# Three moves in VectorE's instruction order: a joining of products, two sums of inputs, and two finishing steps

## The chip, the cores and the metric

The kernel runs on one core of a Trainium2 chip. The time is the device time of one execution in microseconds (us); shorter is better. The median of three runs stands for the kernel.

## The reference

Eight samples of 3008 tokens by 256 channels, all in fp32. Each goes through a filter in the frequency domain along the tokens and then through a mixer of two small networks, one along the tokens and one along the channels.

```python
X = np.fft.rfft(x, axis=1)                      # 8 x 1505 x 256
Y = X * (filt_r + 1j * filt_i)[None]
x = np.fft.irfft(Y, n=3008, axis=1)             # the filter
xt = x.transpose(0, 2, 1)
h = np.maximum(xt @ w_tok1, 0.0) @ w_tok2       # 3008 -> 256 -> 3008, along the tokens
u = x + h.transpose(0, 2, 1)
h2 = np.maximum(u @ w_ch1, 0.0) @ w_ch2         # 256 -> 1536 -> 256, along the channels
out = u + h2
```

## The kernel before

**The filter.** 3008 is 47 times 64, and the Fourier transform is done as matmuls over the factor 64 and then over the factor 47. The samples form the groups (0), (1, 2), (3, 4), (5, 6), (7) (`GROUPS`). The generator `dft(bs)` holds the filter's work for one group and is stopped at every `yield`; the letter that it yields names the step that comes next. Sample 0's filter runs at the start; each later group's runs beside the mixer of the group before it. For the last three groups the steps are these.
- `s`: `x_sums` adds and subtracts the two halves of a loaded pair of input blocks on VectorE (two instructions into the tile `sd`, line 548). The input blocks (`x_pair`, into the tiles `filt`) are loaded ahead: three pairs when the group begins.
- `d`, `c`: `a_pair` is the matmuls by the length-64 table (line 523); the results leave through ScalarE and a transfer.
- `b`: `b_pair` is the matmuls by the length-47 table; `products` multiplies by the filter (line 705).
- `m`: `join` subtracts and adds the products of a pair of frequencies (two VectorE instructions on tile `p`, lines 710 and 711), for the inverse length-47 matmuls `bi_pair` (`i`, or ahead of the next `products`).

**The mixer.** `mix` walks over items (sample `b`, tile `m` of up to 512 tokens, pair `jp` of the hidden blocks): 8 x 6 x 6. The number of an item within its sample is `i % n`, with `n` = 36, so the last six items of a sample (30 to 35) are its tail. An item's matmuls stand in this order on TensorE: `up_first` (four, line 984), `down` part 0 of the item before (three, line 1018), `up_last` (three, line 1000), and `down` parts 1 and 2 (two and two, line 1018). All matrix products are fast schemes with seven products in place of eight, so VectorE makes sums around each: `hh` and `s` in `up_middle`, `t` in `h_sums`, `hh` again in `up_last`, all recorded at line 962 (`v`). A matmul of the item waits for the sums ahead of it, and two PSUM banks (`ps_pg`) serve each item in turn. Each fp32 matmul leaves two records in the trace.

When a tile's six items are through, `finish` gives six VectorE steps (`a`, `b_`, `c`, `d`, a transposition, and a second transposition with the stores of the output). They wait in the list `todo_v`; `one_step` takes one from it. In the first sample a step is taken early in an item, ahead of the sums `t`, and a step later in it; in the other samples two are taken later in the item.

**The token product.** In item 32 of each sample but the last, `token_product` runs the next sample's first token matmul as 12 times seven matmuls (line 850). VectorE prepares the sums `ts` for block `j + 2` when block `j` is done. At its end ScalarE copies a part of the result into the tile `c` (line 856), and VectorE makes three sums into `c` out of PSUM; a fourth, the ReLU (ScalarE, line 865) and five sums on GpSimd (`combine`, lines 378 to 382) follow in item 33. Its first readers on TensorE are the matmuls at line 905 in item 34.

**What sets the order.** The program is written out in the order of these Python calls; each engine runs its own instructions in that order. Within an item `mix` yields at the places 0, 1, 1.5 and 2, and the driver at the end of the kernel lets the filter go on one step where the table `due` names the pair (`jp`, place) for the step that comes next. In a tail the step `m` is due at (2, 2), which is after the token product, and the step `s` at (5, 1) alone; in other items `s` is due at (0, 1), (2, 1), (3, 1) and (5, 1). A new group's filter begins at item 32, place 2, of the first, third and fifth sample; there the three pairs of inputs are asked for. In the second, fourth and sixth sample item 32 has a step `m` at that place.

Of the kernel before, what the change touches and what calls it, by code (L numbers as in the profile page):

```python
# [42 lines left out]
JP = JT // 2  # L43
# [3 lines left out]
MT = 6  # L47
# [4 lines left out]
AP = A // 2  # L52
# [75 lines left out]
def kernel(  # L128
# [712 lines left out]
    def token_product(b):  # L841
        one, two = (bank(tag).rearrange("p (s n) -> p s n", n=P) for tag in turn)
        for j in range(AP):
            w, t = w1_ring[:, j % W1S], token_ts[b][:, j % 2]
            r = 2 * j % TC4
            rows = t4[b, 2 * j // TC4][:, r:r + 2].rearrange("p r (e n) -> p (r e) n", e=DH)
            todo = ((one, 0, 0, rows[:, 0]), (one, 1, 1, rows[:, 2]), (two, 2, 5, rows[:, 3]), (one, 3, 6, t[:, 0]),
                    (two, 0, 4, t[:, 1]), (one, 2, 3, t[:, 2]), (two, 1, 2, t[:, 3]))
            for i, (ps, at, n, mov) in enumerate(todo):
                nc.tensor.matmul(ps[:, at], w[:, n], mov, start=(j == 0 and i in (0, 2)), stop=(j == AP - 1 and i >= 5))  # L850
            if j + W1S < AP:
                w1_load(j + W1S)
            if j + 2 < AP:
                t4_sums(b, j + 2)
        c = rp.tile([P, 8, P], FP32, tag="r", name="c")
        nc.scalar.copy(out=c[:, 0], in_=one[:, 0])
        v(c[:, 1:3], one[:, 1:3], c[:, 0:1].to_broadcast([P, 2, P]))
        v(c[:, 3], two[:, 0], c[:, 2])
        v(c[:, 4:8:3], one[:, 3:4].to_broadcast([P, 2, P]), c[:, 2:4])
        h1 = w2[:, 0:1, 7 * 256:].rearrange("p o (s t) -> p o s t", t=P)[:, :, 0:7, :]  # L860

        def finish_h1():
            v(c[:, 5:7], two[:, 1:3], c[:, 3:5])
            for at, to in ((slice(1, 7, 5), slice(0, 5, 4)), (slice(5, 8, 2), slice(1, 7, 5))):
                nc.scalar.activation(out=h1[:, 0, to, :], in_=c[:, at], func=AF.Relu)
            combine(h1)

        todo_h1.append(finish_h1)
        return h1[:, 0]
# [239 lines left out]
    h1s, uts, vts = {}, {}, {}  # L1109
# [22 lines left out]
    def mix(next_ready):  # L1132

        wait = []
        pos, hhs, tts = {}, {}, {}

        def loads(b):
            if b + 1 < B and next_ready(b):
                for c in wait:
                    t4_load(b + 1, c)  # L1140
                wait.clear()


        own = ({(4, 2): (0, 1)}, {(2, 2): (0,), (3, 0): (1,), (3, 2): (2, 3)})
        new = {(JP - 2, 0): (0, 1), (JP - 1, 0): (2, 3)}

        def u_parts(b, m, jp, place):
            parts = own[b > 0] if m + 1 < MT else new if b + 1 < B else {}
            now = parts.get((jp, place), ())
            b, m = (b, m + 1) if m + 1 < MT else (b + 1, 0)  # L1150
            for part in now:
                u_part(b, m, part)
            if now and now[-1] == max(p for ps in parts.values() for p in ps):
                if m:
                    wait.append(m)
                todo_v.extend(v_steps(b, m))
                if b and (b, m) < (B - 1, MT - 2):
                    w2m_load((m + 2) % MT)

        to_dram = [f for m in range(MT) for f in w2_sums(m)]  # L1160
        w1_todo, w1_out = w1_sums()
        items = [(b, m, jp) for b in range(B) for m in range(MT) for jp in range(JP)]
        n = MT * JP
        for i in range(len(items) + 1):
            now, old = i < len(items), i >= 1
            if not now:
                bo, mo, jo = items[i - 1]
                t = tp.tile([P, 4, 256], FP32, tag="t", name="t")
                last_item(bo, mo, jo, hhs.pop(i - 1), t, uts[bo, mo], pos[bo, mo])
                break  # L1170
            if JP - 2 <= i < JP + 2:
                for _ in range(6 if i > JP - 2 else 1):
                    if w1_todo:
                        w1_todo.pop(0)()
            elif i >= 2 * JP and i % 2 and w1_out:
                w1_out.pop(0)()
            if i and ended[0] < len(tiles):
                convert_middle()
                convert_end(False)
                convert_middle()  # L1180
            if now:
                b, m, jp = items[i]
                if i % n == 0:
                    wait.append(0)
                w = width(m)
                hhs[i] = hp.tile([P, 4, 256], FP32, tag="hh", name="hh")
                g = [bank("pg").rearrange("p (s n) -> p s n", s=2) for _ in range(2)]
                s = up_first(jp, uts[b, m], vts[b, m], w, g)
                up_middle(hhs[i], w, g, s)
            while todo_h1:  # L1190
                todo_h1.pop()()
            if i < n:
                one_step()
            if old:
                bo, mo, jo = items[i - 1]
                tts[i - 1] = tp.tile([P, 4, 256], FP32, tag="t", name="t")
                for f in h_sums(hhs[i - 1], tts[i - 1], width(mo)):
                    f()
                down(mo, jo, 0, hhs[i - 1], tts[i - 1], pos.setdefault((bo, mo), []))
            if now:  # L1200
                u_parts(b, m, jp, 0)
            copies()
            yield b, i % n, 0
            if ended[0] < len(tiles):
                if i == 0:
                    convert_middle()
                convert_end(False)
            if now:
                up_last(jp, uts[b, m], vts[b, m], w, g, s, hhs[i])
                if b + 1 < B and i % n == n - 4:  # L1210
                    t4_sums(b + 1, 0)
            one_step()
            if i >= n or i % n == n - 1:
                one_step()
            if now and b + 1 < B:
                if n - 4 - W1S <= i % n < n - 4:
                    w1_load(i % n - (n - 4 - W1S))
                if i % n == n - 4:
                    t4_sums(b + 1, 1)
            copies()  # L1220
            loads(b)
            yield b, i % n, 1
            if old:
                down(mo, jo, 1, hhs[i - 1], tts[i - 1], pos[bo, mo])
            yield b, i % n, 1.5
            if old:
                down(mo, jo, 2, hhs.pop(i - 1), tts.pop(i - 1), pos[bo, mo])
                if jo == JP - 1:
                    todo_v.extend(finish(bo, mo, uts[bo, mo], pos[bo, mo]))
                    one_step()  # L1230
                    one_step()
            if now:
                if b + 1 < B and i % n == n - 4:
                    h1s[b + 1] = token_product(b + 1)
                u_parts(b, m, jp, 2)
                if jp == JP - 1:
                    while todo_v and m + 1 == MT:
                        one_step()
                if i >= 8 and to_dram:
                    to_dram.pop(0)()  # L1240
                if i in (28, 29):
                    w2m_load(i - 28)
            loads(b)
            yield b, i % n, 2
        while todo_v:
            one_step()

    with tc.manual_schedule():
# [61 lines left out]
        group, todo, done = -1, iter(()), True  # L1310
# [6 lines left out]
        coming = "a"  # L1317
        n = MT * JP
        for b, i, place in mix(next_ready):
            at = (b, i, place)  # L1320
            if at == (0, 0, 0) or group + 1 < len(GROUPS) and at == (GROUPS[group][-1], n - 4, 2):
# [3 lines left out]
                done = group + 1 == len(GROUPS)  # L1325
                todo = iter(()) if done else dft(GROUPS[group + 1]) if group else second
                coming = next(todo, "end") if group else "a"
                if group:
                    continue
            if done:  # L1330
                continue
            jp = i % JP
            if coming in "aw":
                due = place == 1 or (place != 1.5 if group == 0 else coming == "w")
            elif group:
                tail = i >= n - JP
                sums_at = ((5, 1),) if tail else ((0, 1), (2, 1), (3, 1), (5, 1))
                due = (jp, place) in {"s": sums_at, "d": ((1, 1.5), (4, 1.5)), "c": ((2, 0), (5, 0)), "b": ((1, 1.5), (3 if tail else 4, 1.5)), "m": ((2, 2) if tail else (3, 1), (5, 1)),
                                      "i": ((0, 1.5), (3 if tail else 4, 1.5))}[coming]
            else:  # L1340
                due = (jp - (coming == "i")) % JP in ((5, 1, 2, 3) if i < 4 * JP else (5, 0, 1, 2, 3)) and place == {"b": 1, "m": 2, "i": 0}[coming]
# [36 lines left out]
```

## Time and profile before

| what | value |
|---|---|
| median of three runs | 2416.26 us (2415.17 to 2418.65) |
| the profiled execution's own time | 2418.01 us |
| its span, first to last instruction | 2416.2 us, clock granted to TensorE 0.996 |
| TensorE (PE) busy | 2374.1 us, 98% |
| VectorE (DVE) busy | 1942.4 us, 80% |
| ScalarE (ACT), GpSimd (POOL) busy | 690.5 us, 29%; 619.2 us, 26% |
| DMA | 278.65 MB, mean 115 GB/s |

A row of a timeline has the start in us from the span's beginning, the length in us, engine, line, operation, output and inputs by their names in the program, shapes, the number of records merged in it, and in brackets the idle time before it with what ended it. A matmul's end in the trace is modelled, so that two busy rows may hide a pause; the distance between starts is measured. A busy share near 100% therefore doesn't show that TensorE never waits.

### The profile page before, as it was taken

How to read it: one execution, taken by the hardware profiler on the slowest of the kernel's cores; microseconds unless marked ns; L12 is line 12 of the kernel's file. 1: busy time of each engine (PE TensorE's matmuls, PEld its weight loads, DVE VectorE, ACT ScalarE, POOL GpSimd, SP SyncE). 2: the span in 40 equal slices, each digit the busy share in tenths (PEclk: the TensorE clock that was granted, in tenths of full speed). 3: DMA queues.
4: the chain of work that ended last, by engine and by line, in shares of the span. 5: the costliest groups of instructions: out<-in, count | busy, mean ns of one | idle time of the engine just before them, and what ended most of it. 6: DMA issues, size and time to landing. Idle time of an engine off the chain costs nothing.

```text
span 2416.2 us, 35472 instructions
## 1 busy us (share of the span) xinstructions
PE 2374.1 (98%) x12340; PEld 1989.5 (82%) x12340; DVE 1942.4 (80%) x3673; ACT 690.5 (29%) x1339; POOL 619.2 (26%) x1115
## 2 busy tenths in 40 slices
PE   7989999999999999999999999999999999999998
PEld 4656676978888888988888888898888988898887
DVE  7798778777887888777788888877888777777776
ACT  5733322232222222123322222213222222222222
POOL 7476332113111211211121112112212112112121
PEclk8999999999999999999999999999999999999999
DMA  9985545534443223534344222344434111311100
GB/s 213 250 234 166 157 142 179 172 122 122 130 134 98 86 78 91 187 97 138 112 132 125 76 81 83 105 161 128 125 106 146 56 60 37 114 63 31 39 15 21
DMA packets 186011, 278.65 MB, mean 115 GB/s; under 512 B 35101, under 2 KB 122859, under 8 KB 185832
## 3 DMA queue, kind: packets, MB, share of 16 engines
q1 hardware_dynamic: 139544, 212.56, 28.7%
q0 software_dynamic: 34688, 53.83, 8.4%
q10 hardware_dynamic: 11600, 10.00, 1.4%
q8 instruction: 98, 1.61, 0.3%
q14 instruction: 81, 0.66, 0.1%
HBM read 193.52 MB, written 82.72 MB: 114 GB/s over the span
## 4 chain that ended last, share of the span: by engine, by line
PE 87%; DVE 6%; DMA 4%; issue 1%; POOL 1%; ACT 1%; SPq 0%; ACTq 0%; DVEq 0%; POOLq 0%
PE ps_po L1018 34%; PE ps_pg L984 19%; PE ps_pg L1000 14%; PE ps_b L523 4%; PE ps_b L850 3%; PE ps_acc L905 3%; PE ps_acc L850 2%; PE ps_b L905 2%; PE ps_pg L523 2%; PE ps_acc L883 2%; PE ps_b L883 2%; DMA st<-in_moe_w_tok_dram 1%; DVE t L962 1%; DVE hh L962 1%; DVE u L962 1%
## 5 line engine op out<-in xcount | busy, mean ns | idle before, releaser
L1026 POOL DMA_DIRECT2D out_dram<-r x752 | 407.9, 550 | 1611.9 <-issue 1149.2
L962 DVE TENSOR_TENSOR hh<-ps_pg,s 128x512 f32<-128x512 f32 (+3 forms) x864 | 482.4, 586 | 193.2 <-ACT s L987 191.3
L1005 ACT ACTIVATE hh<-hh 128x512 f32<-128x512 f32 (+1 forms) x576 | 347.8, 621 | 975.9 <-DVE hh L962 975.9
L1018 PE MATMUL ps_po<-t,wc 128*128 128x256 f32 (+1 forms) x2296 | 551.5, 379 | 1.8 <-DVE t L962 1.8
L1018 PEld LDWEIGHTS ps_po<-t,wc 128*128 128x128 f32 x2296 | 428.3, 190 | 110.2 <-issue 41.8
L984 PE MATMUL ps_pg<-v,wc 128*128 128x256 f32 (+1 forms) x1728 | 413.4, 376 | 1.7 <-POOL wc L381 1.6
L1018 PE MATMUL ps_po<-hh,wc 128*128 128x256 f32 (+1 forms) x1722 | 412.2, 375 | 0.6 <-POOL wc L382 0.6
L984 PEld LDWEIGHTS ps_pg<-v,wc 128*128 128x128 f32 x1728 | 327.9, 190 | 41.7 <-DVE v L962 3.2
L1018 PEld LDWEIGHTS ps_po<-hh,wc 128*128 128x128 f32 x1722 | 327.0, 190 | 39.4 <-POOL wc L382 1.7
L1000 PE MATMUL ps_pg<-u,wc 128*128 128x256 f32 (+1 forms) x1152 | 294.0, 378 | 1.9 <-DVE hh L962 1.3
L962 DVE TENSOR_TENSOR t<-t,hh 128x256 f32<-128x256 f32 (+1 forms) x576 | 246.2, 427 | 19.8
L1000 PEld LDWEIGHTS ps_pg<-u,wc 128*128 128x128 f32 x1152 | 216.3, 190 | 47.9 <-DVE hh L962 18.2
L962 DVE TENSOR_TENSOR s<-ps_pg,hh 128x512 f32<-128x512 f32 (+1 forms) x288 | 196.1, 681 | 30.7 <-DVE hh L962 0.9
L987 ACT COPY s<-ps_pg 128x256 f32<-128x256 f32 (+1 forms) x288 | 105.9, 368 | 343.6 <-PE ps_pg L984 339.3
L962 DVE TENSOR_TENSOR t<-hh 128x512 f32<-128x512 f32 (+1 forms) x288 | 195.4, 678 | 0.6 <-ACT hh L1005 0.6
L984 PE MATMUL ps_pg<-u,wc 128*128 128x256 f32 (+1 forms) x576 | 169.3, 376 | 2.4 <-DVE hh L962 2.4
L1000 PE MATMUL ps_pg<-v,wc 128*128 128x256 f32 (+1 forms) x576 | 168.9, 375 | 0.0
L984 PEld LDWEIGHTS ps_pg<-u,wc 128*128 128x128 f32 x576 | 108.3, 190 | 18.6 <-DVE hh L962 5.5
L1000 PEld LDWEIGHTS ps_pg<-v,wc 128*128 128x128 f32 x576 | 109.1, 190 | 12.7
L962 DVE TENSOR_TENSOR u<-ps_acc,u 128x256 f32<-128x256 f32 (+1 forms) x84 | 46.2, 550 | 80.4 <-PE ps_acc L905 56.9
L962 DVE TENSOR_TENSOR u<-ps_b,u 128x512 f32<-128x512 f32 (+2 forms) x126 | 74.5, 591 | 28.8 <-PE ps_b L905 26.7
L905 PE MATMUL ps_acc<-w 128*128 128x256 f32 (+1 forms) x336 | 85.3, 376 | 0.0
(164 smaller groups left out, 2638.6 us busy)
## 6 DMA issues: line engine op xcount, KB each, us to landing
w<-w_tmp SPq DMA_DIRECT2D x84, 448.0 KB
w<-w_tmp SPq DMA_DIRECT2D x35, 896.0 KB
out_dram<-r POOLq DMA_DIRECT2D x696, 32.0 KB, 2.2
g_tmp<-t SPq DMA_DIRECT2D x112, 192.0 KB
t<-g_tmp SPq DMA_DIRECT2D x42, 512.0 KB
t<-z_tmp SPq DMA_DIRECT2D x180, 96.0 KB
z_tmp<-t SPq DMA_DIRECT2D x60, 256.0 KB
filt<-in_x_dram SPq DMA_DIRECT2D x90, 128.0 KB
```

The lines of the kernel that those rows point to most:

```text
L523: nc.tensor.matmul(outs(i, j), stat(i, j), mov(i, j), start=True, stop=True)
L850: nc.tensor.matmul(ps[:, at], w[:, n], mov, start=(j == 0 and i in (0, 2)), stop=(j == AP - 1 and i >= 5))
L883: nc.tensor.matmul(ps[:, ds(q * P, n)], t4[b, c][:, r, ts(dh, P)], wai[:, 0:n], start=(first and q == 0), stop=(not first and q == 3))
L905: nc.tensor.matmul(ps[:, ds(j * hw, hw)], h1[:, n, :], w2m[m % 2][:, at, 0:hw], start=(i < 2 and j == 0), stop=(j == len(todo) - 1))
L962: nc.vector.tensor_tensor(out=out, in0=in0, in1=in1, op=op)
L984: nc.tensor.matmul(ps[:, 0:hw], chan[0][:, jp, n, :], mov, start=True, stop=True)
L987: nc.scalar.copy(out=s[:, 0], in_=g[0][:, 0, 0:hw])
L1000: nc.tensor.matmul(ps[:, 0:hw], chan[0][:, jp, n, :], mov, start=True, stop=True)
L1005: nc.scalar.activation(out=hs, in_=hs, func=AF.Relu)
L1018: nc.tensor.matmul(po[i][:, j, 0:hw], chan[1][:, jp, n, :], mov, start=(jp == 0 and first == 1), stop=(jp == JP - 1 and last == 1))
L1026: q.dma_start(bass.AP(tensor=ob.tensor, offset=ob.offset + row * D + g * cw, ap=[[N1 * D, 32], [D if h else -D, n], [1, cw]]), blocks[ts(g ...
```

## The change

Three things are moved, all of them instructions of VectorE. The other engines keep their order, and no instruction is added or taken away.
- The step `m` in the tail stands in the token product, after the last sums `ts` and ahead of the sums into `c`. For this `token_product` becomes a generator with a place 1.7. It acts in the second, fourth and sixth sample.
- The first two steps `s` of a group stand in items 33 and 35, before in item 35 and in item 0 of the next sample. It acts in the first, third and fifth sample.
- In the first sample's items 30 to 35 the steps of `todo_v` are taken two at a time later in the item, as in the other samples. This moves `c` (two sums, `u<-u,r`) of the fifth tile in item 31, and its first transposition in item 32, behind the sums `t` and `hh` of the item.

```diff
@@ token_product @@
             if j + 2 < AP:
                 t4_sums(b, j + 2)
+            if j + 3 == AP:
+                yield b - 1, MT * JP - 4, 1.7
@@ mix @@
-            if i < n:
+            if i < n - JP:
                 one_step()
...
             one_step()
-            if i >= n or i % n == n - 1:
+            if i >= n - JP:
                 one_step()
...
-                    h1s[b + 1] = token_product(b + 1)
+                    h1s[b + 1] = yield from token_product(b + 1)
@@ the driver @@
-            if done:
+            if done or place == 1.7 and coming != "m":
                 continue
...
-                sums_at = ((5, 1),) if tail else ((0, 1), (2, 1), (3, 1), (5, 1))
+                sums_at = ((3, 1), (5, 1)) if tail else ((0, 1), (2, 1), (3, 1), (5, 1))
...
-  "m": ((2, 2) if tail else (3, 1), (5, 1)),
+  "m": ((2, 1.7) if tail else (3, 1), (5, 1)),
```

## The prediction

> **What bounds the kernel now.** I read the page first: the engines' shares and the chain that ended last.
>
> ```profile
> PE 2374.1 (98%) x12340; PEld 1989.5 (82%) x12340; DVE 1942.4 (80%) x3673; ACT 690.5 (29%) x1339; POOL 619.2 (26%) x1115
> PE 87%; DVE 6%; DMA 4%; issue 1%; POOL 1%; ACT 1%; SPq 0%; ACTq 0%; DVEq 0%; POOLq 0%
> ```
>
> TensorE is the bound, and its work is not touched. The change can only win or lose pauses between matmuls. As the ends of matmuls are modelled, I look for pauses in the distances between starts in TensorE's timeline. Undisturbed, a record of 224 columns takes 0.19 us (six in 1.14 us) and one of 256 columns 0.216 us (six in 1.30 us, from rows such as 2172.70 and 2173.99). I compare a tail that has the moved step with a tail that hasn't. First the second sample's item 33, where the joining stands now, on TensorE:
>
> ```profile
> 742.39 1.30 PE L1018 MATMUL ps_po<-hh,wc 128*128 128x224 f32 x6
> 743.99 1.02 PE L1000 MATMUL ps_pg<-u,wc 128*128 128x224 f32 x4 [0.30 <-DVE hh L962]
> 744.85 0.54 PE L1000 MATMUL ps_pg<-v,wc 128*128 128x224 f32 x2
> 745.58 1.02 PE L1018 MATMUL ps_po<-t,wc 128*128 128x224 f32 x4 [0.19 <-DVE t L962]
> ```
>
> The same rows in the third sample, whose tail has no joining:
>
> ```profile
> 1028.65 1.30 PE L1018 MATMUL ps_po<-hh,wc 128*128 128x224 f32 x6
> 1029.79 0.92 PE L1000 MATMUL ps_pg<-u,wc 128*128 128x224 f32 x4
> 1030.92 1.68 PE L1018 MATMUL ps_po<-t,wc 128*128 128x224 f32 x8
> ```
>
> From the first to the last of these starts it is 3.19 us with the joining and 2.27 us without. VectorE's timeline at the place says why:
>
> ```profile
> 741.15 0.43 DVE L962 TENSOR_TENSOR c<-ps_b,c 128x256 f32<-128x256 f32 x1 [2.43 <-ACT c L856]
> ...
> 742.35 0.68 DVE L710 TENSOR_TENSOR p<-p,p 128x512 f32<-128x512 f32 x1
> 742.95 0.68 DVE L711 TENSOR_TENSOR p<-p,p 128x512 f32<-128x512 f32 x1
> 743.55 0.38 DVE L962 TENSOR_TENSOR hh<-ps_pg,s 128x224 f32<-128x224 f32 x1
> ```
>
> VectorE is idle for 2.43 us ahead of `c`, and then 1.20 us of joining (742.35 to 743.55) stands ahead of the sum that frees the bank for the matmul at 743.99. In the third sample that sum follows the `c` sums at once.
>
> For the other two moves, VectorE's timeline in the first sample's tail, and TensorE's:
>
> ```profile
> 428.83 0.75 DVE L962 TENSOR_TENSOR u<-u,r 128x256 f32<-128x256 f32 x2
> 429.50 0.62 DVE L962 TENSOR_TENSOR t<-hh 128x448 f32<-128x448 f32 x1
> ...
> 462.74 0.39 DVE L962 TENSOR_TENSOR hh<-ps_pg,s 128x224 f32<-128x224 f32 x1 [1.27 <-ACT s L987]
> ...
> 482.57 1.28 DVE L548 TENSOR_TENSOR sd<-filt 128x512 f32<-128x512 f32 x2
> ...
> 485.72 0.42 DVE L962 TENSOR_TENSOR hh<-ps_pg,s 128x256 f32<-128x256 f32 x1
> ```
>
> ```profile
> 429.10 0.54 PE L1000 MATMUL ps_pg<-v,wc 128*128 128x224 f32 x2
> 430.26 1.75 PE L1018 MATMUL ps_po<-t,wc 128*128 128x224 f32 x8 [0.62 <-DVE t L962]
> ...
> 482.67 0.59 PE L984 MATMUL ps_pg<-u,wc 128*128 128x256 f32 x2
> ...
> 484.53 1.53 PE L1018 MATMUL ps_po<-hh,wc 128*128 128x256 f32 x6
> ...
> 486.19 1.13 PE L1000 MATMUL ps_pg<-u,wc 128*128 128x256 f32 x4
> ...
> 487.68 1.10 PE L1018 MATMUL ps_po<-t,wc 128*128 128x256 f32 x4
> ```
>
> At 430.26 a `down` waits 0.78 us (429.10 plus two records is 429.48) for a `t` that stands behind two finishing sums. Around 485 three small waits follow on the pair's sums at 482.57, which hold up the finishing sums and `hh`.
>
> **The joining (three samples).** Two instructions go from behind `c` into the idle time ahead of it. The last `ts` sum starts at 738.43 and is over by 738.72; the joining takes 1.20 us, to about 739.9, and `c` can't start before 741.15, when ScalarE's copy is there. So it costs nothing in its new place, and would cost only from the point where that 2.43 us of idle shrank under 1.20. Its inputs are products of item 31's stretch, done long before on VectorE itself. In the old place the third sample's pattern returns: 3.19 - 2.27 = 0.92 us, and the 0.10 us by which the first record pair after a pause is stretched (four records of the row at 745.58 take 0.95 us, not 0.76, of which 0.09 belongs to the filter's matmuls after it) is gone too: 1.02 us. The fourth and sixth sample show the same pauses to 0.01 us (1315.08 and 1885.84). Sum: 3 x 1.02 = 3.06 us. Next late are the matmuls of `b_pair`, whose banks are freed by the fourth `c` sum, which moves forward by the same 1.2 us.
>
> **The pairs' sums (three samples).** In item 35 the same work stays (the second pair's sums instead of the first's); item 36 loses 1.20 us. The seventh sample's tail has no sums at all: there TensorE goes from the same `up_first` (2172.26) to the same `down` (2176.58) in 4.32 us, against 487.68 - 482.67 = 5.01 here. With the restart of 0.08 us that is 0.77 us. The one pair left in item 35 makes VectorE about 0.3 us later at 478.85 than in the seventh sample; there VectorE then idles 0.40 us for a ScalarE copy (2172.85), which takes that up. Sum: 3 x 0.77 = 2.30 us (the third and fifth sample show the same waits at 1057.29 and 1628.39).
>
> The first pair's sums come new into item 33, behind `hh` at 460.32 to 461.46. They need 1.20 us, VectorE is idle there for 1.27 us: 461.39 + 1.20 = 462.59, and `hh` starts at 462.74 anyway. What could stretch them is GpSimd, which makes its `combine` sums just then (461.43 and 461.97, 0.46 us each, until 462.43; the same distance from `c` in the third and fifth sample). The row for this: a joining at 399.82 that ran beside two such sums of GpSimd took 1.03 and 1.21 us instead of 0.68, together 0.88 more. With 0.88 us, or at most twice 0.46 = 0.92, the `hh` of item 34 would come 0.75 us late. It then has 0.22 us idle ahead of `u` at 465.46, and the bank that its second sum frees at 467.68 is needed at 468.37, with 0.14 us from an end to the matmul released by it (430.12 to 430.26): 0.55 us more. So the stretch is just covered; I price it at 0, with 0.3 us each, 0.9 in all, as the upper end, and no gain below 0, since nothing waits for these sums before item 37.
>
> The Trainium skill, page "SBUF — State Buffer", section "Who interferes with whom", says that a VectorE instruction with two SBUF inputs and a GpSimd instruction that reads SBUF exclude each other for the whole instruction, and that the order of issue decides who waits. This rule speaks against the new place, and the stretched joining agrees with it. By it alone, with both GpSimd sums served first, my estimate is the same 0.9 us of delay, and the sum of the gains would be 6.1 or 5.2 us according to whether the cover holds.
>
> The moved sums are also a new wait: VectorE stops for the six transfers of the pair two items earlier. Behind it in VectorE's queue stand `hh`, `s`, `t` of item 34, and for those waits TensorE. SP issued the first pair from 445.71 on and the last of all three at 457.38, and DMA is idle (share 0.00) from 460 to 462; in the third sample the last is issued at 1027.35 and the share is 0.03 from 1029 on for a need at 1032.5, in the fifth 1599.41, and 0.00 from 1602 for 1603.6. Cost: 0.
>
> **The finishing steps (first sample only).** The two `u<-u,r` sums cost 0.67 us (428.83 to 429.50) ahead of `t`. Without them `t` is there at 429.45, its matmul can start at 429.59 against a wish of 429.48: of 0.78 us, 0.11 stay. Gain 0.67 us. Behind `hh` they end at about 432.6 as before, since the whole amount of work is the same; the next `hh` started at 433.24 after 0.61 us of idle. The transposition's move in item 32 frees 0.63 us ahead of `t` where TensorE doesn't wait; the stores follow the second transposition, which keeps its time, and so does GpSimd's queue. I take 0.7 us, between 0.5 and 0.9.
>
> **The sum.** 3.06 + 2.30 + 0.67 = 6.0 us: span 2416.2 to 2410.2. The profiled execution took 2418.01, 1.75 above the median of 2416.26; the same loss applied to the median gives 2410.2. With the bounds, the gain is between 5.0 (GpSimd's stretch uncovered) and 6.3; runs of before lie 1.1 below and 2.4 above their median. A change under about 0.2%, 4.8 us, can't be told from none; the forecast is 0.25%.
>
> **Rivals.** *The pairs' sums return nothing*: the sums of item 33, slowed by GpSimd, make `hh` late by more than its cover, and what item 36 wins is lost in items 34 and 35. For it: the overlap with GpSimd is certain. Against: the cover of 0.92 us. Gain 3.06 + 0.67 = 3.7: 2412.5 us. Chance 0.12.
>
> *The pauses only move*: TensorE, earlier by a microsecond, meets a wait of fixed time further on, such as a transfer. Against: in the page's waits TensorE and VectorE have almost no DMA among their releasers in the mixer. About 2415.8 us. Chance 0.04.
>
> *Slower, by the transfer wait*: the first pair's inputs land late at item 33 in three samples, and VectorE, in order, holds `hh` of item 34. Each microsecond beyond 0.92 us of cover counts three times; it eats the whole gain when the data is 0.92 + 6.0 / 3 = 2.9 us late, and at 4 us it costs 9.2 - 6.0 = 3.2: 2419.5 us. Against: the transfers are over 1.4 to 3 us before the need. Chance 0.04.
>
> **How the numbers follow.** My forecast has 0.80; 0.70 of this lies beyond 0.2% and 0.10 within it through the scatter of runs. The first rival gives 0.04 to faster and 0.08 to the same, the second is the same. Faster 0.74, same 0.22, slower 0.04. The range from 2408.2 to 2413.0 takes in the bounds, the scatter and the first rival.
>
> **What would show it.** In the changed profile: the pauses ahead of `up_last` and `down` in item 33 of the second, fourth and sixth sample are gone, and the joining starts directly after the last `ts`; the run from `up_first` to `down` at item 37 takes 4.3 us in the first, third and fifth sample; the wait before `down` in item 31 is about 0.1 us. The `sd` sums of item 33 may take up to 1 us longer. I am wrong if TensorE pauses in items 34 or 35 of those samples, or if VectorE shows an idle time ended by a transfer there.

## The result, and the profile after

The changed kernel takes 2411.65 us (median of 20 runs, 2407.93 to 2413.63), the kernel before 2417.9 us beside it (20 runs, 2414.1 to 2419.79). The ratio is 0.9975 with a 95% interval from 0.9969 to 0.9981: 6.25 us less, and clear of no change. The profiled execution took 2410.47 us, its span is 2408.7 us. The forecast of 2410.2 us stood on a median of 2416.26 us from three runs, 1.6 us under the one from twenty; the forecast gain was 6.0 us.

The same lines of the page as before; the line numbers behind `token_product` are two higher:

```profile
PE 2370.9 (98%) x12340; PEld 1988.3 (83%) x12340; DVE 1941.2 (81%) x3673; ACT 690.2 (29%) x1339; POOL 622.6 (26%) x1115
PE 90%; DVE 4%; DMA 3%; issue 1%; ACT 1%; POOL 1%; SPq 0%; ACTq 0%; DVEq 0%; POOLq 0%
```

The work is the same, and VectorE's share of the chain that ended last falls from 6% to 4%: less of that chain runs through its instructions. Only GpSimd's busy time has grown, by 3.4 us; 2.4 us of this are the two stretched sums shown below, in three samples.

The second sample's item 33 on TensorE:

```profile
739.52 1.30 PE L1020 MATMUL ps_po<-hh,wc 128*128 128x224 f32 x6
740.66 0.92 PE L1002 MATMUL ps_pg<-u,wc 128*128 128x224 f32 x4
...
741.79 0.92 PE L1020 MATMUL ps_po<-t,wc 128*128 128x224 f32 x4
```

From the first to the last start it is 2.27 us, as in the third sample before; it was 3.19. VectorE at the place:

```profile
735.77 0.68 DVE L710 TENSOR_TENSOR p<-p,p 128x512 f32<-128x512 f32 x1
736.37 0.69 DVE L711 TENSOR_TENSOR p<-p,p 128x512 f32<-128x512 f32 x1
738.28 0.42 DVE L964 TENSOR_TENSOR c<-ps_b,c 128x256 f32<-128x256 f32 x1 [1.23 <-ACT c L858]
...
739.48 0.38 DVE L964 TENSOR_TENSOR hh<-ps_pg,s 128x224 f32<-128x224 f32 x1
```

The joining has taken 1.20 of the 2.43 us of idle; `c` still waits for ScalarE, and `hh` follows the `c` sums.

The first sample's tail, VectorE and then TensorE:

```profile
427.41 0.62 DVE L964 TENSOR_TENSOR t<-hh 128x448 f32<-128x448 f32 x1
...
459.24 1.54 DVE L548 TENSOR_TENSOR sd<-filt 128x512 f32<-128x512 f32 x2
460.71 0.38 DVE L964 TENSOR_TENSOR hh<-ps_pg,s 128x224 f32<-128x224 f32 x1
...
481.43 0.39 DVE L964 TENSOR_TENSOR r<-ps_po,r 128x224 f32<-128x224 f32 x1 [0.40 <-ACT r L1080]
...
482.87 0.41 DVE L964 TENSOR_TENSOR hh<-ps_pg,s 128x256 f32<-128x256 f32 x1
```

```profile
427.69 0.54 PE L1002 MATMUL ps_pg<-v,wc 128*128 128x224 f32 x2
428.18 1.75 PE L1020 MATMUL ps_po<-t,wc 128*128 128x224 f32 x8
...
480.53 0.59 PE L986 MATMUL ps_pg<-u,wc 128*128 128x256 f32 x2
...
482.25 1.46 PE L1020 MATMUL ps_po<-hh,wc 128*128 128x256 f32 x6
483.55 1.03 PE L1002 MATMUL ps_pg<-u,wc 128*128 128x256 f32 x4
...
484.85 1.08 PE L1020 MATMUL ps_po<-t,wc 128*128 128x256 f32 x4
```

Item 31's `down` starts 0.49 us after the pair of records ahead of it (0.38 would be none lost). From 480.53 to 484.85 it is 4.32 us, as in the seventh sample of the kernel before, whose tail has no pair's sums:

```profile
2172.26 0.59 PE L984 MATMUL ps_pg<-u,wc 128*128 128x256 f32 x2
...
2176.58 1.89 PE L1018 MATMUL ps_po<-t,wc 128*128 128x256 f32 x8
```

As there, VectorE idles 0.40 us for ScalarE, here at 481.43. The pair's sums in item 33 took 1.47 us of VectorE's time (459.24 to 460.71) instead of 1.20, beside these on GpSimd:

```profile
459.29 0.94 POOL L381 TENSOR_TENSOR w<-w 128x128 f32<-128x128 f32 x1
460.31 0.79 POOL L382 TENSOR_TENSOR w<-w 128x128 f32<-128x128 f32 x1
```

In the kernel before:

```profile
461.43 0.46 POOL L381 TENSOR_TENSOR w<-w 128x128 f32<-128x128 f32 x1
461.97 0.46 POOL L382 TENSOR_TENSOR w<-w 128x128 f32<-128x128 f32 x1
```

The `hh` of item 34 starts 6.53 us behind the first `c` sum (454.18), where it was 6.42 us: 0.11 us late.

**The gain by stretches.** VectorE's first `c` sum of each of the seven tails is a good mark: TensorE's work between two marks is the same in every kernel here, so their distance is that work and its pauses. The first column runs from a matmul of item 31's `up_first` (426.35 in the kernel before) to the first mark.

| us | item 31 to 1st | 1st to 2nd | 2nd to 3rd | 3rd to 4th | 4th to 5th | 5th to 6th | 6th to 7th | to the end |
|---|---|---|---|---|---|---|---|---|
| before | 29.98 | 284.83 | 286.26 | 284.83 | 286.27 | 284.49 | 262.92 | 270.32 |
| changed | 29.25 | 284.10 | 285.08 | 284.10 | 285.09 | 283.76 | 261.89 | 270.48 |
| joining alone | 29.97 | 284.84 | 285.10 | 284.84 | 285.10 | 284.49 | 261.90 | 270.37 |
| pairs' sums alone | 29.98 | 284.13 | 286.27 | 284.13 | 286.27 | 283.77 | 262.91 | 270.32 |
| finishing alone | 29.26 | 284.85 | 286.27 | 284.84 | 286.27 | 284.47 | 262.91 | 270.43 |
| sums twice | 29.25 | 284.82 | 285.10 | 284.84 | 285.45 | 284.49 | 261.88 | 270.49 |
| late transfer | 29.25 | 292.78 | 285.10 | 291.15 | 285.10 | 291.51 | 261.89 | 269.84 |
| sums in item 34 | 29.25 | 284.12 | 285.10 | 284.11 | 285.10 | 283.77 | 261.89 | 270.49 |
| later pairs too | 29.26 | 283.14 | 285.10 | 283.04 | 285.10 | 283.41 | 261.89 | 270.39 |

Where a kernel does the same, the distances agree within some hundredths of a us in different executions; this tells gains apart that the medians can't. Of the changed kernel's gain, 0.73 us is in item 31, 3 x 0.73 = 2.19 in the tails with the pairs' sums, and 1.18 + 1.18 + 1.03 = 3.39 in those with a joining: 6.3 us. The last stretch is 0.16 us longer, but there two executions of one kernel differ by 0.14 us (270.39 and 270.53 for the later pairs), so that I count it neither as a loss nor as none. The span fell by 7.5; the remaining 1.4 us lies ahead of 426.35, where the two kernels have the same instructions in the same order, and is chance (below).

### The profile page after: what moved, and what is told of

Same layout as the page of the kernel before. It is cut to its first block, busy times and chain, and to the rows that moved or that the text cites. A ratio compares the mean times of both kernels' runs of the same rounds, so it can differ in the third digit from the quotient of the medians.

```text
span 2408.7 us, 35472 instructions
## 1 busy us (share of the span) xinstructions
PE 2370.9 (98%) x12340; PEld 1988.3 (83%) x12340; DVE 1941.2 (81%) x3673; ACT 690.2 (29%) x1339; POOL 622.6 (26%) x1115
## 4 chain that ended last, share of the span: by engine, by line
PE 90%; DVE 4%; DMA 3%; issue 1%; ACT 1%; POOL 1%; SPq 0%; ACTq 0%; DVEq 0%; POOLq 0%
PE ps_po L1020 34%; PE ps_pg L986 19%; PE ps_pg L1002 15%; PE ps_b L523 4%; PE ps_b L850 3%; PE ps_acc L907 3%; PE ps_acc L850 2%; PE ps_b L907 2%; PE ps_pg L523 2%; PE ps_b L885 2%; PE ps_acc L885 2%; DMA st<-in_moe_w_tok_dram 1%; DVE t L964 1%; DVE hh L964 1%; DMA filt<-in_filt_r_dram 0%
```

## The experiments

**The parts one by one.** The first kernel has the joining in its new place and the other two moves undone:

```diff
-                sums_at = ((3, 1), (5, 1)) if tail else ((0, 1), (2, 1), (3, 1), (5, 1))
+                sums_at = ((5, 1),) if tail else ((0, 1), (2, 1), (3, 1), (5, 1))
...
-            if i < n - JP:
+            if i < n:
                 one_step()
...
-            if i >= n - JP:
+            if i >= n or i % n == n - 1:
                 one_step()
```

> The joining alone. My theory: the pauses ahead of the matmuls of item 33 go in the second, fourth and sixth sample, 1.0 us each and up to 1.15 with the bank of the following matmuls, 3.1 to 3.4 us in all; the distance between the first sums into c of neighbouring samples shrinks by that much across those samples (286.26 to about 285.1 us) and stays elsewhere (284.84 us across samples three and five). Rival 'the pauses only move': the distances stay within 0.2 us of before and the time too.

Measured: 2415.15 us against 2418.36, ratio 0.9984 (0.9975 to 0.9993), and the distances fall by 1.16, 1.17 and 1.02 us where the joining is and nowhere else: 3.35 us. The joining is the largest part, and its pauses do not move elsewhere.

The second has the pairs' sums alone, on the kernel before:

```diff
-                sums_at = ((5, 1),) if tail else ((0, 1), (2, 1), (3, 1), (5, 1))
+                sums_at = ((3, 1), (5, 1)) if tail else ((0, 1), (2, 1), (3, 1), (5, 1))
```

> The pairs' sums alone. My theory: 0.73 us less in the first, third and fifth sample's tails, 2.2 us in all, the other distances as before (286.26 us). Rival 'the pairs' sums return nothing': no change in those distances, with pauses in items 34 and 35 in place of items 36 and 37.

Measured: 2416.55 us against 2418.36, ratio 0.9991 (0.9982 to 0.9999); the three distances fall by 0.70, 0.70 and 0.72 us, 2.1 in all. The rival that these sums return nothing is out.

The third has the finishing steps alone, on the kernel before:

```diff
-            if i < n:
+            if i < n - JP:
                 one_step()
...
-            if i >= n or i % n == n - 1:
+            if i >= n - JP:
                 one_step()
```

> The finishing steps alone, first sample only. My theory: the pause ahead of down in item 31 falls from 0.78 to 0.11 us and nothing else changes: 0.7 us, at the edge of what can be told. Rival: the sums behind hh make the next hh late, and the pause comes back in item 32: no change in the sum of pauses over items 31 and 32.

Measured: 2418.47 us against 2418.36, ratio 1.0 (0.9992 to 1.0009), so the time alone shows nothing. The trace shows it: 29.98 falls to 29.26 us, 0.72, and the distances between the marks stay within 0.02 us. The three parts add to 3.35 + 2.12 + 0.72 = 6.2 us, against 6.3 in the whole change.

**Does the overlap with GpSimd cost TensorE anything?** The first pair's sums of a group are put in item 34, away from GpSimd's sums:

```diff
-                sums_at = ((3, 1), (5, 1)) if tail else ((0, 1), (2, 1), (3, 1), (5, 1))
+                sums_at = ((4, 1), (5, 1)) if tail else ((0, 1), (2, 1), (3, 1), (5, 1))
```

> The whole change, with the first pair's sums in item 34 instead of 33, away from GpSimd's sums. VectorE idles 1.55 us there ahead of the next hh, and the sums need 1.2. My theory: the overlap with GpSimd in item 33 costs TensorE nothing, so the distances between samples stay within 0.1 us of the changed kernel's (284.10 us across samples one, three and five). Rival: the overlap costs, and the distances shrink by 0.2 us or more each.

Measured, one execution: 2410.01 us, and the distances agree with the changed kernel's within 0.02 us. Here VectorE's pair takes 1.28 us and GpSimd's two sums 0.46 us each, as in the kernel before. The overlap stretches VectorE's and GpSimd's sums and costs TensorE nothing.

**How much is covered in item 33?** The first pair's sums are made twice:

```diff
-        for e, op in enumerate((ALU.add, ALU.subtract)):
+        for e, op in ((0, ALU.add), (1, ALU.subtract)) * times:
...
-                sds.append(x_sums(*todo[j], j))
+                sds.append(x_sums(*todo[j], j, 2 if j == 0 else 1))
```

> The whole change, with the first pair's sums of a group made twice in item 33 (four instructions, the second time the same values into the same tile). My theory, cover: 2.4 us of sums and 0.3 us lost to GpSimd against 1.35 us of idle make hh of item 34 1.3 us late; 0.77 us of that is covered, so TensorE pauses about 0.5 us per sample ahead of item 35's first matmuls, 1.6 us in all. Rival, no cover: the late hh goes to TensorE in full, 1.3 us per sample or more, ahead of item 34's up_last.

Measured, one execution: 2413.31 us, and the three distances are 0.72, 0.74 and 0.73 us longer than the changed kernel's, 2.2 in all where I expected 1.6. The third sample's tail, VectorE and then TensorE:

```profile
1029.45 3.01 DVE L548 TENSOR_TENSOR sd<-filt 128x512 f32<-128x512 f32 x4
1032.38 0.38 DVE L964 TENSOR_TENSOR hh<-ps_pg,s 128x224 f32<-128x224 f32 x1
```

```profile
1034.92 1.68 PE L1020 MATMUL ps_po<-t,wc 128*128 128x224 f32 x8
1037.05 0.65 PE L986 MATMUL ps_pg<-u,wc 128*128 128x224 f32 x2 [0.45 <-DVE hh L964]
```

`hh` stands 8.00 us behind the first `c` sum instead of 6.42 us in the kernel before: 1.58 us late, where I expected 1.3, because two of the four sums meet GpSimd's and take 0.94 us, not one. TensorE goes on through item 34 without a pause and waits ahead of item 35, by 2.13 us for eight records that take 1.51: 0.62 us and 0.11 of restart, which is the distance's 0.74 us but for 0.01. So 0.96 us of the lateness was covered, where I had 0.77 us. The place is the one expected; the rival without cover expected item 34. The fourth to fifth distance also shows 0.35 us more, in pauses ahead of `up_last` and `down` some 32 us behind the fourth mark. VectorE idles 0.46 us between `hh` and `s` (1334.71) ahead of them, where the changed kernel's `s` follows after 0.11 us; the cause stays open.

**The price of a late transfer.** The three pairs that open a group are asked for a second time in reverse order:

```diff
-            for i, u in to_load[0:n]:
+            for i, u in to_load[0:n] + (to_load[0:n][::-1] if tiled and n == FB else []):
                 (x_pair if tiled else x_load)(*u, i, queue)
```

> The whole change, with the three pairs of inputs that open a group asked for a second time in reverse order, so that the first pair lands last. This tries the price of the transfer rival. In the changed kernel the transfers end about 1 to 3 us ahead of the need; as many again, at about 12 us for three pairs, end some 8 us after it. Theory of in-order waiting: VectorE idles about 8 us in item 33 of the first, third and fifth sample, ended by a transfer, and all but 0.9 us of it reaches TensorE: 3 x 7 = 21 us more than the changed kernel. Rival: VectorE's wait is covered by TensorE's other matmuls up to the need of the sums in item 37: under 1 us.

A row of VectorE's timeline, rows of TensorE's, a row of VectorE's waits (us in total, times, the longest), and a stretch with TensorE's granted clock (the number after the five engines):

```profile
471.32 1.29 DVE L548 TENSOR_TENSOR sd<-filt 128x512 f32<-128x512 f32 x2 [8.87 <-DMA filt<-in_x_dram]
```

```profile
465.85 1.03 PE L907 MATMUL ps_b<-w 128*128 128x256 f32 x4
472.97 1.86 PE L1002 MATMUL ps_pg<-u,wc 128*128 128x224 f32 x4 [6.09 <-DVE hh L964]
474.62 0.95 PE L1002 MATMUL ps_pg<-v,wc 128*128 128x224 f32 x2
```

```profile
DVE sd L548 <- DMA filt<-in_x_dram: 23.0, 3, 8.9
```

```profile
473.00:478.00 5.00, 5.00 (x14) 4.56 (x15) 4.46 (x9) 0.82 (x2) 0.00 (x0) 0.53 0.00 0
```

Measured, one execution: 2436.46 us, and 8.68, 7.05 and 7.75 us more than the changed kernel in the three distances, 23.5 in all, where I expected 21. The sums are a wait in VectorE's order, and `hh` of item 34 behind them brings it to TensorE. The changed kernel has no such idle time because its inputs land earlier, not because the wait is harmless. The size has a second source: after 6.1 us without a matmul the granted clock is 0.53, and four records take 1.65 us (472.97 to 474.62) instead of 0.76. Of the 8.68 us, 6.26 are the longer wait ahead of 472.97, and 2.4 are the slow records behind it. What the wait alone would have cost isn't shown, since slow matmuls also cover later waits.

**One step further.** In the changed kernel the same pattern was left over in five places: the first sums of a later pair in item 5, the second in item 0, ahead of the finishing sums. Here both stand in item 5:

```diff
-                sums_at = ((3, 1), (5, 1)) if tail else ((0, 1), (2, 1), (3, 1), (5, 1))
+                sums_at = ((3, 1), (5, 1)) if tail else ((2, 1), (3, 1), (5, 1))
...
+                if coming == "s" and not tail and due and jp == 5:
+                    due = 2
```

> The whole change, and the later pairs' sums too leave item 0: both stand in item 5 (five times in the kernel). In the changed kernel's trace the matmuls of item 1 after them pause by 0.17 + 0.10 + 0.09 = 0.36 us, with the same cause as in the tails (sums ahead of the finishing sums). If VectorE's idle time in item 5 and the cover of 0.55 us hold the 1.2 us more, 5 x 0.36 = 1.8 us less than the changed kernel, 0.33% under the kernel before. Rival: item 5 and 0 have 2.1 us of idle for 2.4 us of sums, so that hh of item 0 comes 0.3 us late and a new pause of up to 0.3 us takes back most of it: as the changed kernel within 0.5 us.

Measured: 2410.9 us (six runs), ratio 0.9966 (0.9953 to 0.9979). One of its six times, 10142.38 us, is far from all others; its granted clock was 0.229 where the others had 0.995 or more, and no cause is known. It did not come back in the repeat. The repeat stands beside the changed kernel on one chip:

> The changed kernel again, beside the next one on the same chip: 6.1 us under the kernel before in the stretch behind the first 425 us, and as much in the median.

> The kernel with the later pairs' sums in item 5 again, for its time beside the changed kernel's on the same chip. In the traces it was 1.0, 1.05 and 0.27 us shorter between the samples. If that is its whole effect, its median lies 2.3 us under the changed kernel's; if something else takes it back, the medians agree within 0.5 us.

Measured: the changed kernel 2412.03 us, ratio 0.9971 (0.9962 to 0.9981); with the later pairs moved 2408.83 us (five runs), ratio 0.9962 (0.9949 to 0.9975). The intervals overlap, and the medians alone would not settle it; the distances do: 283.14, 283.04 and 283.41 against 284.13, 284.13 and 283.77 in the changed kernel beside it, 2.4 us less (2.3 in the first trace of this version), where I first expected 1.8. The new pause of the rival isn't there. TensorE in item 1 behind the first such pair, in the changed kernel and then in this one:

```profile
527.65 1.46 PE L1020 MATMUL ps_po<-hh,wc 128*128 128x256 f32 x6
529.11 1.13 PE L1002 MATMUL ps_pg<-u,wc 128*128 128x256 f32 x4
530.08 0.59 PE L1002 MATMUL ps_pg<-v,wc 128*128 128x256 f32 x2
530.60 1.10 PE L1020 MATMUL ps_po<-t,wc 128*128 128x256 f32 x4
```

```profile
528.45 1.46 PE L1020 MATMUL ps_po<-hh,wc 128*128 128x256 f32 x6
529.74 1.03 PE L1002 MATMUL ps_pg<-u,wc 128*128 128x256 f32 x4
530.61 0.59 PE L1002 MATMUL ps_pg<-v,wc 128*128 128x256 f32 x2
531.04 1.03 PE L1020 MATMUL ps_po<-t,wc 128*128 128x256 f32 x4
```

From the first to the last of these starts 2.95 us become 2.59: the 0.36 us that I expected of a place. Behind them the last `down` and the filter's matmuls take 0.07 and 0.10 us less, which I hadn't counted. In VectorE's timeline four sums stand in a row and the 0.36 us of idle ahead of the finishing sum `r` is back:

```profile
520.02 2.49 DVE L548 TENSOR_TENSOR sd<-filt 128x512 f32<-128x512 f32 x4
...
527.31 0.42 DVE L964 TENSOR_TENSOR r<-ps_po,r 128x256 f32<-128x256 f32 x1 [0.36 <-ACT r L1080]
```

This version has the shortest distances of the study.

## Why the prediction was right

**Comparing tails.** The reading that carried the sum, a tail with the moved step against a tail without it, held to the hundredth: 3.19 fell to 2.27 us and 5.01 to 4.32.

**The joining.** Forecast 3 x 1.02, measured 1.18, 1.18 and 1.03. The first two were undersized by 0.16 us. I had stopped the comparison at item 33's `down`; behind it, in the second and fourth sample, the inverse matmuls of `bi_pair` into the banks `ps_pg` also waited a little for the late `hh`, and the joining alone takes 0.15 us off there. In the second sample, the kernel before and then the changed one:

```profile
746.53 0.65 PE L523 MATMUL ps_b<-t,wb 48*64 48x512 f32 x2
...
748.56 0.65 PE L1018 MATMUL ps_po<-t,wc 128*128 128x224 f32 x2
```

```profile
742.64 0.65 PE L523 MATMUL ps_b<-t,wb 48*64 48x512 f32 x2
...
744.52 1.02 PE L1020 MATMUL ps_po<-t,wc 128*128 128x224 f32 x4
```

2.03 us become 1.88. In the sixth sample the inverse matmuls at the place go into other banks (`ps_b` and `ps_acc`), and 1.03 is the forecast. That the new place is free is shown by the 1.23 us of idle left ahead of `c`.

**The pairs' sums.** Forecast 3 x 0.77, measured 0.73 in the changed kernel and 0.70 to 0.72 alone. I had counted a restart of 0.08 us as gone with the pauses; 0.05 us of it stays, since the row at 484.85 still takes 0.05 us more than the four records and the filter's start need (1.00 us to the next row; four records of 0.216 us and 0.09 for the filter's start make 0.95).

**GpSimd.** The overlap is there, but the loser was named wrongly in the bound. I let VectorE wait for both GpSimd sums, 0.88 us; it lost 0.27, and GpSimd 0.81 (0.94 + 0.79 against 2 x 0.46). VectorE's first sum began at 459.24, ahead of GpSimd's at 459.29, and took its usual 0.68 us; its second, at 459.84, took 0.94. So the engine that began first went on undisturbed, which agrees with the rule on the order of issue cited in the prediction. The row at 399.82 was a poor measure for this place. On VectorE and GpSimd in the kernel before:

```profile
399.82 1.03 DVE L710 TENSOR_TENSOR p<-p,p 128x512 f32<-128x512 f32 x1
400.77 1.21 DVE L711 TENSOR_TENSOR p<-p,p 128x512 f32<-128x512 f32 x1
```

```profile
400.59 0.83 POOL L943 TENSOR_TENSOR w<-w 128x256 f32<-128x256 f32 x1
401.51 1.06 POOL L932 TENSOR_TENSOR w<-w 128x256 f32<-128x256 f32 x1
```

GpSimd's sums there are of 256 elements, not 128, so they aren't the same sums as I had taken them to be. The second of VectorE's began behind a sum of GpSimd; the first began ahead of it and was stretched all the same, and what stretched it isn't shown. How much of the difference between 0.88 and 0.27 us is the size of GpSimd's sums and how much the order was not tested. Neither cost TensorE anything, as the sums in item 34 show.

**The finishing steps.** Forecast 0.67 us, measured 0.73 and 0.72 alone; 0.11 us of the pause stays, as worked out. So the terms were off by +0.3 us (the joining), -0.1 (the pairs' sums) and +0.06: the mechanism held in all three, and that the sum came within 0.3 us of the 6.3 in the distances is in small part luck, as the two larger errors have opposite signs.

**The cover.** Twice the sums showed 0.96 us where the prediction had 0.77; the term for the time from VectorE's end to the matmul was taken at 0.14 us, and the matmul at 1037.05 starts 0.05 us after `hh` ends (1036.38 and 0.62 us), so 0.09 us of the difference is this; the other 0.10 us is not accounted for.

**The rivals.** "Return nothing" fell with the second and the sums-in-item-34 kernel, "the pauses only move" with the first. The slower rival did not come about, because the transfers were early; its price was set too low. By it, idle time less 0.92 us of cover, the late-transfer kernel's three idle times of 8.87, 6.66 and 7.44 us come to 20.2 us, and 23.5 were measured: it left out the slow clock behind a long pause.

## What to carry to other kernels

When the busiest engine shows 98%, go by the distance between its starts and not by its busy share: 6 us of time to be won lay in seven places of 0.7 to 1.2 us each, much of it hidden behind modelled ends. To price a moved instruction, find the same stretch of the same program without that instruction and subtract; and follow the comparison until the next resource that the late instruction frees, not only to the first matmul that waits. A step belongs into idle time that another engine sets, as here the 2.43 us in which VectorE waits for ScalarE's copy, provided that its inputs are there, since in an engine that works in order it is a wait for everything behind it.

## What the runs showed of the hardware that was not expected

**A pause costs more than its length.** In the late-transfer kernel, 6.1 us without a matmul were followed by a stretch of 5 us with a granted clock of 0.53, and the next stretch had 1.00 again. The Trainium skill, page "TensorE: Matmul & The Clock Gate", section "Part 1: The HAM clock gate", says that after an idle window of about 3.4 us the array gets half its clock until it has been busy for about as long; this trace agrees: 0.53 over 5 us is half the clock for some 4.7 of them (my estimate), with matmuls in all of that time.

**The scatter ahead of 426.35, and shorter pauses.** The matmul that stands at 426.35 in the kernel before stands between 424.40 and 429.08 in the eleven profiled executions, though the instructions ahead of it are the same; behind it, like distances agree within some hundredths of a us. At about 111 us TensorE waits for a transfer ahead of the first token matmuls. In the kernel before it waited 0.95 us and the clock stayed; in the kernel with the joining alone it waited 2.85 us:

```profile
111.53 6.74 PE L799 MATMUL ps_b<-t,w 128*128 128x256 f32 x16 [2.85 <-DMA t<-g_tmp]
```

The stretch from 111 to 115 us, in the kernel before and then in that one:

```profile
111.00:115.00 4.00, 4.00 (x19) 3.54 (x20) 3.74 (x10) 0.49 (x2) 2.41 (x5) 1.00 1.00 198
```

```profile
111.00:115.00 4.00, 3.47 (x8) 2.87 (x9) 2.48 (x5) 0.00 (x0) 2.74 (x6) 0.50 1.03 185
```

The clock is at half behind the longer wait: 8 records in place of 19 in these 4 us, of which 0.53 us went by before they began. The wait is longer mostly because TensorE came to it earlier (its last matmul ahead ends at 108.68 us by the trace, in the kernel before at 110.05). Of the eleven profiled executions, four waited 2.42 to 2.85 us here, and all four lost clock; seven waited 0.91 to 1.53 us, and none did. So here a pause under the page's 3.4 us, as the trace marks pauses, was enough; how long it must be, and why, was not tested. The four have the matmul of 426.35 at 427.66 to 429.08, the seven at 424.40 to 427.08. The wait thus goes with a part of the scatter; the seven still differ by 2.7 us without it. This is read from traces only; no kernel was run to take the wait away.
